# Running the first half of a GEGLU FFN beside a block convolution, with streamed weights, batched complex products and a second PSUM buffer for FFN2

## Chip, cores, metric

One core of one Trainium2 chip. The metric is the device time of one execution in microseconds (us); where several runs of a kernel are quoted, it is their median. Runs are marked fast or slow by their own spread; only fast ones are compared, except one single run (e3_serial_b) whose state is unknown and which is named as such.

## The reference, cut to what matters

The inputs are bf16: u of 2048 tokens by D = 640 channels, SSM parameters of 640 by 128, FFN weights with F = 1728. The FFN reads u too; its own x is not used.

```python
g = sigmoid((u * gate_w).sum(-1, keepdims=True))
# a: state-space layer as a long convolution
K = real(einsum("dn,dnl,dn->dl", C, exp(dt * A * l), dt * B))    # 640 x 2048
a = irfft(rfft(pad(u)) * rfft(pad(K)))[:2048] + u * Dskip
# b: GEGLU feed-forward
b = (gelu(u @ w_gate) * (u @ w_up)) @ w_down                     # tanh form of gelu
return g * a + (1 - g) * b
```

## The kernel before

It has five stages, one after another: the SSM kernel K (80 pieces); DFT tables and the forward DFT of K in four blocks of 512; the convolution, block by block in the frequency domain; FFN1 (56 tiles of up to 128 features by 512 tokens); FFN2 with the final mix (16 tiles of 128 tokens). A complex spectrum has nine planes of 640 columns: real and imaginary planes alternate, and plane 8 is the Nyquist plane. The parts that the change and the argument touch:

```python
K_sb = kpool.tile([128, TC, D], BF16, name="K_sb")            # K stays in SBUF
Kf = big.tile([128, NB, NT, D], BF16, name="Kf")              # and so do all its spectra
...
for c in range(NB):                                           # convolution, output block c of 4
    ub = upool.tile([128, 4, D], BF16, name="ub")
    nc.sync.dma_start(out=ub[:], in_=u2[c * S:(c + 1) * S, :].rearrange("(t p) d -> p t d", p=128))
    ...
    fwd_block(ub, lambda k: k, Uf, c)                         # DFT: TensorE, copied out by ScalarE
    for i in range(c + 1):
        j = c - i
        for t in range(4):                                    # one complex plane at a time
            Ur = Uf[:, i, 2 * t, :]; Ui = Uf[:, i, 2 * t + 1, :]
            Kr = Kf[:, j, 2 * t, :]; Ki = Kf[:, j, 2 * t + 1, :]
            ...                                               # 8 products and sums of 128x640
    ...                                                       # Mc = Sprev * sgn + Sc, VectorE
    for mo in range(4):
        pY = psY.tile([128, D], FP32, name="pY")              # inverse DFT of Mc on TensorE
        ...
        nc.vector.tensor_tensor(out=a_sb[:, tcx, :], in0=a_sb[:, tcx, :], in1=pY[:], op=ALU.add)

# FFN: everything is loaded only here, in tiles that reuse the convolution's memory
xT = fp.tile([128, nkt, L], BF16, name="xT")
for kt in range(nkt):
    nc.sync.dma_start_transpose(out=xT[:, kt, :], in_=u2[:, kt * 128:(kt + 1) * 128])
nc.sync.dma_start(out=Wg[:], in_=B_w_gate.rearrange("(k p) f -> p k f", p=128))
nc.sync.dma_start(out=Wu[:], in_=B_w_up.rearrange("(k p) f -> p k f", p=128))
...
for ft in range(nft):                                         # FFN1
    for tq in range(L // 512):
        ...                                                   # 5 + 5 matmuls, then
        nc.scalar.copy(out=Gs[:fsz], in_=pGt[:fsz])
        nc.scalar.copy(out=Us[:fsz], in_=pUt[:fsz])
        nc.vector.tensor_tensor(out=q[:fsz], in0=Gs[:fsz], in1=Gs[:fsz], op=ALU.mult)
        nc.vector.tensor_scalar(out=q[:fsz], in0=q[:fsz], scalar1=0.044715, scalar2=1.0, op0=ALU.mult, op1=ALU.add)
        nc.vector.tensor_tensor(out=q[:fsz], in0=q[:fsz], in1=Gs[:fsz], op=ALU.mult)
        nc.scalar.activation(out=sg[:fsz], in_=q[:fsz], func=ACT.Sigmoid, scale=GELU_C)
        nc.vector.tensor_tensor(out=sg[:fsz], in0=sg[:fsz], in1=Gs[:fsz], op=ALU.mult)
        nc.vector.tensor_tensor(out=HT[:fsz, ft, toks], in0=sg[:fsz], in1=Us[:fsz], op=ALU.mult)
for tt in range(TC):                                          # FFN2
    pD = psF.tile([128, D], FP32, name="pD", bufs=1)
    ...                                                       # 28 matmuls, b_sb on ScalarE, mix on VectorE
```

Of the kernel before, what the change touches and what calls it, by code (L numbers as in the profile page):

```python
# [9 lines left out]
ALU = mybir.AluOpType  # L10
ACT = mybir.ActivationFunctionType
FP32 = mybir.dt.float32
# [10 lines left out]
def kernel(  # L23
# [73 lines left out]

    kctx = ExitStack()
    kctx.__enter__()
    kpool = kctx.enter_context(tc.tile_pool(name="kpool", bufs=1))  # L100
    K_sb = kpool.tile([128, TC, D], BF16, name="K_sb")

    with ExitStack() as k1:
# [171 lines left out]
        def kgen_contract_C(hb, tabs):  # L275
# [11 lines left out]
            for r in range(4):  # L287
                nc.sync.dma_start(out=K_sb[32 * r:32 * (r + 1), :, cslc],
                                  in_=K0[:, r:X2:4, :])
# [28 lines left out]
    if "K" in dbg:  # L318
        nc.sync.dma_start(out=dbg["K"].rearrange("(j p) d -> p j d", p=128), in_=K_sb[:])
    persist = kctx.enter_context(tc.tile_pool(name="persist", bufs=1))  # L320
    a_sb = persist.tile([128, TC, D], BF16, name="a_sb")
    g_sb = persist.tile([128, TC], BF16, name="g_sb")
    with ExitStack() as k2:
# [7 lines left out]

        dctx = ExitStack()
# [60 lines left out]
        dctx.__exit__(None, None, None)  # L393
        Uf = big.tile([128, NB, NT, D], BF16, name="Uf")
        Kf = big.tile([128, NB, NT, D], BF16, name="Kf")
        dchs = [(0, 512), (512, D - 512)] if D > 512 else [(0, D)]

        def fwd_block(src, kidx, spec, b):
            for mt in range(NT):
                pU = psT.tile([128, D], FP32, name="pU")  # L400
                for (d0, dn) in dchs:
                    for k in range(4):
                        nc.tensor.matmul(pU[:, d0:d0 + dn], lhsT=FW[:, k, mt, :], rhs=src[:, kidx(k), d0:d0 + dn],  # L403
                                         start=(k == 0), stop=(k == 3))
                nc.scalar.copy(out=spec[:, b, mt, :], in_=pU[:])  # L405

        for b in range(NB):
            fwd_block(K_sb, lambda k, b=b: 4 * b + k, Kf, b)

        upool = k2.enter_context(tc.tile_pool(name="ublk", bufs=2))  # L410
        spool = k2.enter_context(tc.tile_pool(name="sacc", bufs=2))
        psY = k2.enter_context(tc.tile_pool(name="psinv", bufs=2, space=bass.MemoryType.PSUM))
        Sprev = None
        for c in range(NB):
            ub = upool.tile([128, 4, D], BF16, name="ub")
            nc.sync.dma_start(out=ub[:], in_=u2[c * S:(c + 1) * S, :].rearrange("(t p) d -> p t d", p=128))
            for k in range(4):
                nc.vector.tensor_tensor(out=a_sb[:, 4 * c + k, :], in0=ub[:, k, :], in1=dsk[:], op=ALU.mult)
            fwd_block(ub, lambda k: k, Uf, c)
            Sc = spool.tile([128, NT, D], BF16, name="Sc")  # L420
            first = True
            for i in range(c + 1):
                j = c - i
                for t in range(4):
                    Ur = Uf[:, i, 2 * t, :]
                    Ui = Uf[:, i, 2 * t + 1, :]
                    Kr = Kf[:, j, 2 * t, :]
                    Ki = Kf[:, j, 2 * t + 1, :]
                    Sr = Sc[:, 2 * t, :]
                    Si = Sc[:, 2 * t + 1, :]  # L430
                    tmp = wk.tile([128, D], BF16, name="ptmp")
# [16 lines left out]
                U8 = Uf[:, i, 8, :]  # L448
                K8 = Kf[:, j, 8, :]
                S8 = Sc[:, 8, :]  # L450
                tmp8 = wk.tile([128, D], BF16, name="ptmp8")
                if first:
                    nc.vector.tensor_tensor(out=S8, in0=U8, in1=K8, op=ALU.mult)
                else:
                    nc.vector.tensor_tensor(out=tmp8[:], in0=U8, in1=K8, op=ALU.mult)
                    nc.vector.tensor_tensor(out=S8, in0=S8, in1=tmp8[:], op=ALU.add)
                first = False
            if c > 0:
                Mc = spool.tile([128, NT, D], BF16, name="Mc", bufs=1)
                for mt in range(NT):  # L460
                    nc.vector.scalar_tensor_tensor(out=Mc[:, mt, :], in0=Sprev[:, mt, :],  # L461
                                                   scalar=sgn[:], in1=Sc[:, mt, :],
                                                   op0=ALU.mult, op1=ALU.add)
            else:
                Mc = Sc
            for mo in range(4):
                pY = psY.tile([128, D], FP32, name="pY")
                for (d0, dn) in dchs:
                    for kt in range(NT):
                        nc.tensor.matmul(pY[:, d0:d0 + dn], lhsT=FI[:, kt, mo, :], rhs=Mc[:, kt, d0:d0 + dn],  # L470
                                         start=(kt == 0), stop=(kt == NT - 1))
                tcx = 4 * c + mo
                nc.vector.tensor_tensor(out=a_sb[:, tcx, :], in0=a_sb[:, tcx, :], in1=pY[:], op=ALU.add)
            Sprev = Sc

    if "a" in dbg:
        nc.sync.dma_start(out=dbg["a"].rearrange("(t p) d -> p t d", p=128), in_=a_sb[:])
    with ExitStack() as k3:
        fp = k3.enter_context(tc.tile_pool(name="ffn", bufs=1))
        fwk = k3.enter_context(tc.tile_pool(name="fwork", bufs=2))  # L480
        psF = k3.enter_context(tc.tile_pool(name="psffn", bufs=2, space=bass.MemoryType.PSUM))
        psC = k3.enter_context(tc.tile_pool(name="psconst", bufs=1, space=bass.MemoryType.PSUM))

        nkt = D // 128
        nft_full = F // 128
        f_last = F - nft_full * 128
        nft = nft_full + (1 if f_last else 0)
        xT = fp.tile([128, nkt, L], BF16, name="xT")
        for kt in range(nkt):
            nc.sync.dma_start_transpose(out=xT[:, kt, :], in_=u2[:, kt * 128:(kt + 1) * 128])  # L490
        Wg = fp.tile([128, nkt, F], BF16, name="Wg")
        nc.sync.dma_start(out=Wg[:], in_=B_w_gate.rearrange("(k p) f -> p k f", p=128))
        Wu = fp.tile([128, nkt, F], BF16, name="Wu")
        nc.sync.dma_start(out=Wu[:], in_=B_w_up.rearrange("(k p) f -> p k f", p=128))
# [4 lines left out]
        gwc = fp.tile([128, nkt], BF16, name="gwc")  # L499
        nc.sync.dma_start(out=gwc[:], in_=gate_w.rearrange("(k p) -> p k", p=128))  # L500

        pG = psC.tile([128, TC], FP32, name="pgate")
        for tt in range(TC):
            for kt in range(nkt):
                nc.tensor.matmul(pG[:, tt:tt + 1], lhsT=xT[:, kt, tt * 128:(tt + 1) * 128], rhs=gwc[:, kt:kt + 1],
                                 start=(kt == 0), stop=(kt == nkt - 1))
        glog = fwk.tile([128, TC], BF16, name="glog")
        nc.scalar.copy(out=glog[:], in_=pG[:])
        nc.scalar.activation(out=g_sb[:], in_=glog[:], func=ACT.Sigmoid)
        if "g" in dbg:  # L510
            nc.sync.dma_start(out=dbg["g"].rearrange("(t p) -> p t", p=128), in_=g_sb[:])
        if "Uf" in dbg:
            pass

        HT = fp.tile([128, nft, L], BF16, name="HT")
        GELU_C = 2.0 * math.sqrt(2.0 / math.pi)
        for ft in range(nft):
            fsz = 128 if ft < nft_full else f_last
            f0 = ft * 128
            for tq in range(L // 512):  # L520
                toks = slice(tq * 512, (tq + 1) * 512)
                pGt = psF.tile([128, 512], FP32, name="pGt")
                pUt = psF.tile([128, 512], FP32, name="pUt")
                for kt in range(nkt):
                    nc.tensor.matmul(pGt[:fsz, :], lhsT=Wg[:, kt, f0:f0 + fsz], rhs=xT[:, kt, toks],  # L525
                                     start=(kt == 0), stop=(kt == nkt - 1))
                for kt in range(nkt):
                    nc.tensor.matmul(pUt[:fsz, :], lhsT=Wu[:, kt, f0:f0 + fsz], rhs=xT[:, kt, toks],  # L528
                                     start=(kt == 0), stop=(kt == nkt - 1))
                Gs = fwk.tile([128, 512], BF16, name="Gs")  # L530
                nc.scalar.copy(out=Gs[:fsz], in_=pGt[:fsz])  # L531
                Us = fwk.tile([128, 512], BF16, name="Us")
                nc.scalar.copy(out=Us[:fsz], in_=pUt[:fsz])  # L533
                q = fwk.tile([128, 512], BF16, name="q")
                nc.vector.tensor_tensor(out=q[:fsz], in0=Gs[:fsz], in1=Gs[:fsz], op=ALU.mult)
# [56 lines left out]
```

## Time and profile before

Four runs before the prediction: 834.88 us (833.73 to 836.83). The table by stage, the chain and their reading stand in the prediction. In short: the convolution is full of VectorE work, FFN1 of TensorE work, and between them lies a hole of 26.6 us in which x and the FFN weights are loaded.

A row of the table by stage reads: stretch, its length, the busy time of TensorE, its weight loads, VectorE, ScalarE and GpSimd (instructions in brackets), the granted TensorE clock, the DMA share, GB/s. In the traces PE is TensorE, DVE is VectorE, ACT is ScalarE, and SPq is the queue of DMA issues on SyncE.

### The profile page before, as it was taken

The page shows a single profiled execution, that of the slowest core. Times are in us where ns is not written, and L with a number is a line of the kernel's source. Part 1 is how long each engine was busy: PE and PEld are TensorE (multiplying, and loading weights), DVE is VectorE, ACT ScalarE, POOL GpSimd, SP SyncE. Part 2 cuts the span into 40 slices and gives each one's busy share as a digit, 9 for nine tenths or more (in the row PEclk, how much of TensorE's full clock was granted, in tenths as well). Part 3 has the DMA queues.
Part 4 walks back from the last instruction along what each step waited for, and adds up shares of the span by engine and source line. Part 5 has one row for each costly group of instructions (what it writes and reads, how often), then busy time and mean ns, then how long its engine had stood idle before and what let it go on. Part 6 is the DMA issues. An engine that isn't in the chain of part 4 may idle for free.

```text
span 833.4 us, 9851 instructions
## 1 busy us (share of the span) xinstructions
PE 509.7 (61%) x3597; PEld 252.2 (30%) x3652; DVE 670.7 (80%) x1580; ACT 456.6 (55%) x560; POOL 5.8 (1%) x25
## 2 busy tenths in 40 slices
PE   0056545755675565316979960500539999998886
PEld 0021313322332323303545530200214444444443
DVE  6979899899999898699979999999417788884333
ACT  1139999999999999525753420000016766661111
POOL 2000000000000000000000000000000000000000
PEclk9998779786976796667999995755859999999999
DMA  2000000000000000100011100000391000000000
GB/s 63 0 0 0 1 1 14 13 4 10 14 13 1 13 13 0 27 13 1 2 64 32 33 1 0 0 0 0 73 322 52 1 1 1 0 1 32 33 32 31
DMA packets 44656, 19.06 MB, mean 23 GB/s; under 512 B 37248, under 2 KB 43328, under 8 KB 44608
## 3 DMA queue, kind: packets, MB, share of 16 engines
q1 hardware_dynamic: 44608, 18.44, 8.6%
q8 instruction: 28, 0.46, 0.2%
q14 instruction: 20, 0.16, 0.1%
HBM read 9.91 MB, written 2.62 MB: 15 GB/s over the span
## 4 chain that ended last, share of the span: by engine, by line
DVE 40%; ACT 35%; PE 17%; issue 3%; DMA 2%; SPq 2%; ACTq 0%; DVEq 0%
PE pD L549 8%; ACT c L267 4%; ACT e L254 4%; ACT c L265 4%; ACT p L269 4%; ACT sg L539 4%; DVE sg L540 3%; DVE Mc L461 3%; DVE q L537 2%; ACT p L268 2%; ACT c L266 2%; PE pY L470 2%; DVE HT L541 2%; DMA Wu<-in_B_w_up_dram 2%; ACT L249 2%
## 5 line engine op out<-in xcount | busy, mean ns | idle before, releaser
L531 ACT CAST Gs<-pGt 128x512 bf16<-128x512 f32 (+1 forms) x56 | 32.2, 577 | 128.3 <-PE pGt L525 127.9
L257 DVE TENSOR_SCALAR kM<-pph 128x512 f32<-128x512 f32 x120 | 79.5, 682 | 22.3 <-PE pph L253 14.5
L525 PE MATMUL pGt<-xT,Wg 128*128 128x512 bf16 (+1 forms) x269 | 70.2, 386 | 24.9 <-DMA Wg<-in_B_w_gate_dram 22.1
L470 PE MATMUL pY<-Mc,FI 128*128 128x128 bf16 (+1 forms) x211 | 36.7, 324 | 78.8 <-DVE Mc L461 78.3
L258 DVE SCALAR_TENSOR_TENSOR p<-kM,pph 128x512 bf16<-128x512 f32 x120 | 77.8, 675 | 0.2
L549 PE MATMUL pD<-Wd,HT 128*128 128x128 bf16 (+3 forms) x440 | 68.0, 298 | 13.1 <-ACT b_sb L552 12.6
L253 PE MATMUL pph<-RX,b_bf 128*128 128x512 bf16 x80 | 36.3, 461 | 60.4 <-DVE p L258 60.2
L528 PE MATMUL pUt<-xT,Wu 128*128 128x512 bf16 (+1 forms) x280 | 69.2, 379 | 0.4 <-ACT Us L533 0.4
L403 PEld LDWEIGHTS <-FW 128*128 128x128 bf16 x576 | 46.5, 101 | 70.4 <-ACT FW L385 26.9
L283 PEld LDWEIGHTS <-c 128*32 128x32 bf16 x640 | 44.7, 104 | 62.5 <-DVE K L285 37.7
L283 PE MATMUL psK<-c,c 128*32 128x64 bf16 x640 | 52.2, 204 | 17.6 <-DVE c L272 12.1
L403 PE MATMUL pU<-K_sb,FW 128*128 128x128 bf16 (+1 forms) x282 | 43.7, 311 | 28.1 <-ACT FW L385 25.3
L539 ACT ACTIVATE sg<-q 128x512 bf16<-128x512 bf16 (+1 forms) x56 | 35.2, 629 | 35.5 <-DVE q L537 35.1
L470 PEld LDWEIGHTS <-FI 128*128 128x128 bf16 x288 | 23.6, 101 | 102.0 <-DVE Mc L461 49.2
L285 DVE CAST K<-psK 32x512 bf16<-32x512 f32 x80 | 51.2, 670 | 3.3 <-PE psK L284 2.9
L556 DVE TENSOR_TENSOR diff<-a_sb,b_sb 128x640 f32<-128x640 bf16 x16 | 13.2, 824 | 50.4 <-ACT b_sb L552 50.4
L284 PE MATMUL psK<-p,p 128*32 128x64 bf16 x640 | 51.5, 203 | 3.1 <-DVE p L273 3.1
L549 PEld LDWEIGHTS <-HT 128*128 128x128 bf16 x448 | 34.7, 97 | 46.6 <-issue 22.3
L405 ACT CAST Uf<-pU 128x640 bf16<-128x640 f32 x36 | 24.9, 692 | 42.9 <-PE pU L403 42.9
L254 ACT ACTIVATE e<-pa 128x512 bf16<-128x512 f32 x80 | 44.5, 595 | 6.6 <-PE pa L252 6.3
L552 ACT CAST b_sb<-pD 128x640 bf16<-128x640 f32 x16 | 11.0, 690 | 66.4 <-PE pD L549 66.4
L284 PEld LDWEIGHTS <-p 128*32 128x32 bf16 x640 | 45.1, 104 | 6.3 <-issue 6.3
(167 smaller groups left out, 1150.0 us busy)
## 6 DMA issues: line engine op xcount, KB each, us to landing
K_sb<-K SPq DMA_DIRECT2D x40, 64.0 KB, 2.3
ub<-in_A_u_dram SPq DMA_DIRECT2D x4, 640.0 KB, 4.2
out_dram<-o_sb SPq DMA_DIRECT2D x16, 160.0 KB, 1.8
Wg<-in_B_w_gate_dram SPq DMA_DIRECT2D x1, 2160.0 KB, 8.6
Wu<-in_B_w_up_dram SPq DMA_DIRECT2D x1, 2160.0 KB, 13.5
Wd<-in_B_w_down_dram SPq DMA_DIRECT2D x1, 2080.0 KB, 19.0
dsk<-in_A_Dskip_dram SPq DMA_DIRECT2D x1, 160.0 KB, 3.6
Are<-in_A_A_re_dram SPq DMA_DIRECT2D x1, 160.0 KB, 3.7
```

The source lines that it names most:

```text
L254: nc.scalar.activation(out=et[:, :, xs], in_=pa[:], func=ACT.Exp)
L257: nc.vector.tensor_scalar(out=kM[:], in0=tau_src, scalar1=MAGIC, scalar2=None, op0=ALU.add)
L258: nc.vector.scalar_tensor_tensor(out=pt[:, :, xs], in0=kM[:], scalar=-MAGIC, in1=tau_src, op0=ALU.add, op1=ALU.subtract)
L283: nc.tensor.matmul(psK[:, ci, :], lhsT=c1[:, dl, :], rhs=c2[:, dl, :], start=True, stop=False)
L284: nc.tensor.matmul(psK[:, ci, :], lhsT=p1[:, dl, :], rhs=p2[:, dl, :], start=False, stop=True)
L285: nc.vector.tensor_copy(out=K0[:, :, ch8 * 8:(ch8 + 1) * 8], in_=psK[:].rearrange("p c x -> p x c"))
L403: nc.tensor.matmul(pU[:, d0:d0 + dn], lhsT=FW[:, k, mt, :], rhs=src[:, kidx(k), d0:d0 + dn], start=(k == 0), stop=(k == 3))
L470: nc.tensor.matmul(pY[:, d0:d0 + dn], lhsT=FI[:, kt, mo, :], rhs=Mc[:, kt, d0:d0 + dn], start=(kt == 0), stop=(kt == NT - 1))
L525: nc.tensor.matmul(pGt[:fsz, :], lhsT=Wg[:, kt, f0:f0 + fsz], rhs=xT[:, kt, toks], start=(kt == 0), stop=(kt == nkt - 1))
L528: nc.tensor.matmul(pUt[:fsz, :], lhsT=Wu[:, kt, f0:f0 + fsz], rhs=xT[:, kt, toks], start=(kt == 0), stop=(kt == nkt - 1))
L539: nc.scalar.activation(out=sg[:fsz], in_=q[:fsz], func=ACT.Sigmoid, scale=GELU_C)
L549: nc.tensor.matmul(pD[:, d0:d0 + dn], lhsT=HT[:fsz, ft, toks], rhs=Wd[:fsz, ft, d0:d0 + dn], start=(ft == 0), stop=(ft == nft - 1))
```

## The change

The intent is to place the TensorE-bound FFN1 beside the VectorE-bound convolution, and so to hide its matmuls and its load. What is needed for that is memory: K and its spectra go to DRAM and come back block by block; the FFN weights are loaded in tiles, once for each quarter of the tokens; H, the result of FFN1, goes to DRAM as well. Besides, the four planes of a complex product are done in one instruction, and FFN2 gets two PSUM buffers. The core of the diff (cuts marked with ...):

```diff
+    K_dram = dram.tile([TC, 128, D], BF16, name="K_dram")
+    Kf_dram = dram.tile([NB, 128, NT, D], BF16, name="Kf_dram")
+    HT_dram = dram.tile([F, L], BF16, name="HT_dram")
-    K_sb = kpool.tile([128, TC, D], BF16, name="K_sb")
...
-                for t in range(4):
-                    Ur = Uf[:, i, 2 * t, :]
...
+        def conv_gen():
...
+                RE = slice(0, 8, 2)
+                IM = slice(1, 8, 2)
+                for i in range(c + 1):
+                    Kfj = kfs.tile([128, NT, D], BF16, name="Kfj", tag="kf")
+                    nc.sync.dma_start(out=Kfj[:], in_=Kf_dram[j])
+                    Ur = Uf[:, i, RE, :]
+                    ...                    # the same products, on 128 x 4 x 640
+                    yield
...
+        def ffn1_gen():
+            for tq in range(L // 512):
+                ...                        # xq: transposed tokens of this quarter; gate
+                yield
+                for ft in range(nft):
+                    if ft % 2 == 0:
+                        ...                # wg2, wu2: 640 x 256 of each weight, two buffers
+                    ...                    # 5 + 5 matmuls into one pGU, one copy of 1024 to GU
+                    ...                    # the same five VectorE instructions and the sigmoid
+                    nc.sync.dma_start(out=HT_dram[f0:f0 + fsz, toks], in_=ht[:fsz])
+                    yield
+        run_interleaved([conv_gen(), two_at_a_time(ffn1_gen())])
...
         for tt in range(TC):
-            pD = psF.tile([128, D], FP32, name="pD", bufs=1)
+            HTs = hp.tile([128, nft, 128], BF16, name="HTs")
+            ...                            # HTs from HT_dram, 256 B runs
+            pD = psD.tile([128, D], FP32, name="pD")      # psD has bufs=2
```

`run_interleaved` takes one step of each generator in turn, so two FFN1 tiles stand beside each step of the convolution. The compiler's scheduler orders each engine's instructions from there.

## The prediction

> **What bounds the kernel now.** I read the page's busy row and slices first, then the busy time of every engine by stage, then the chain, then the groups of the stages that the change touches, and last the DMA issues.
>
> ```profile
> PE 509.7 (61%) x3597; PEld 252.2 (30%) x3652; DVE 670.7 (80%) x1580; ACT 456.6 (55%) x560; POOL 5.8 (1%) x25
> DVE 40%; ACT 35%; PE 17%; issue 3%; DMA 2%; SPq 2%; ACTq 0%; DVEq 0%
> ```
>
> The first line is the share of busy time, the second the chain that ended last. No engine bounds the whole span. The stages run one after another, each with its own limit, which the table by stage shows (stretch, its length, busy us per engine, TensorE clock, DMA share, GB/s):
>
> ```profile
> 0.00:354.60 354.60, 185.59 (x1681) 90.24 (x1700) 307.05 (x429) 288.45 (x229) 5.76 (x25) 0.82 0.07 11
> 354.60:425.30 70.70, 43.69 (x282) 23.53 (x288) 70.25 (x477) 40.01 (x107) 0.00 (x0) 0.81 0.03 5
> 425.30:595.80 170.50, 86.33 (x566) 46.23 (x576) 161.89 (x364) 25.60 (x37) 0.00 (x0) 0.76 0.05 16
> 595.80:622.40 26.60, 4.60 (x14) 1.78 (x15) 1.91 (x4) 1.16 (x2) 0.00 (x0) 0.62 0.97 272
> 622.40:752.20 129.80, 125.70 (x644) 57.85 (x654) 101.99 (x277) 90.99 (x171) 0.00 (x0) 1.00 0.05 16
> 752.20:833.40 81.20, 63.77 (x413) 32.52 (x419) 27.61 (x33) 10.41 (x16) 0.00 (x0) 1.00 0.09 33
> ```
>
> Row 1 makes the SSM kernel K (ScalarE and VectorE bound). Row 2 makes the DFT tables (VectorE 70.25 of 70.70) with the forward DFT of K beside them on TensorE. Row 3 is the block convolution: VectorE is busy 161.89 of 170.50 and TensorE only half. Row 4 is a hole: every engine waits for x and the FFN weights, DMA share 0.97. Row 5 is FFN1, bound by TensorE (125.70 of 129.80) with VectorE at 101.99. Row 6 is FFN2, where TensorE waits. So a VectorE-bound stage stands before a TensorE-bound one, with a load between.
>
> The groups of the convolution and of FFN1 that I count with:
>
> ```profile
> L272 DVE TENSOR_TENSOR c<-c,e 128x4096 bf16<-128x4096 bf16 x10 | 22.9, 2289 | 4.0 <-ACT c L267 3.9
> L270 DVE TENSOR_TENSOR c<-c,e 128x2048 bf16<-128x2048 bf16 x10 | 12.2, 1221 | 2.3 <-ACT c L266 1.8 <-ACT e L249 0.5
> L446 DVE TENSOR_TENSOR ptmp<-Uf,Kf 128x640 bf16<-128x640 bf16 x24 | 11.1, 481 | 0.0
> L461 DVE SCALAR_TENSOR_TENSOR Mc<-Sc,sgn 128x640 bf16<-128x640 bf16 x27 | 21.8, 876 | 0.0
> L525 PE MATMUL pGt<-xT,Wg 128*128 128x512 bf16 (+1 forms) x269 | 70.2, 386 | 24.9 <-DMA Wg<-in_B_w_gate_dram 22.1 <-ACT Gs L531 2.0
> L552 ACT CAST b_sb<-pD 128x640 bf16<-128x640 f32 x16 | 11.0, 690 | 66.4 <-PE pD L549 66.4
> ```
>
> And three pieces of the timeline: two products that start 0.80 us apart per pair, and one FFN2 tile, where TensorE idles 0.82 us for its only pD buffer.
>
> ```profile
> 491.50 0.80 DVE ptmp L440 x2
> 788.22 4.28 PE L549 MATMUL pD<-Wd,HT 128*128 128x512 bf16 x27 [0.82 <-ACT b_sb L552]
> 829.86 0.88 DVE L558 SCALAR_TENSOR_TENSOR o_sb<-diff,g_sb,b_sb 128x640 bf16<-128x640 f32 x1
> ```
>
> **What the Trainium skill says.** (1) "VectorE: DVE Perf Modes", The perf-mode tier table: a bf16 tensor_tensor reaches two elements per cycle and no more. The trace agrees: from 128x2048 to 128x4096 the time grows by 1068 ns for 2048 elements, 0.521 ns each. (2) Same page, What auto-detection actually checks: this mode asks for 16-bit tensors with step 1. The new products read four planes of 640 with a stride between; the inner step stays 1, so I keep the mode, though no instruction of this trace has that shape. (3) "TensorE: Matmul & The Clock Gate", Part 1: idle stretches throttle the array, sustained work releases it. The trace agrees: 0.76 granted in the convolution, 1.00 in FFN1. (4) "DMA: Bandwidth & Descriptors", Specifications: transfers want runs of at least 512 B. The new weight tiles have 512 B runs, the new HTs loads 256 B. No transfer of these shapes is in the trace; the nearest is K_sb, 64 KB in 128 B runs, 2.3 us to landing.
>
> **The change part by part.**
>
> *Stages 1 and 2* keep their VectorE and ScalarE work and order. K goes to DRAM in place of SBUF and is read back in blocks; the read (two DMAs of a few us after the last K piece) lies under the 20 us in which the tables are not ready anyway. The first four FFN1 tiles can use TensorE's idle time there, and the first u block no longer has a late load (4.0 us of VectorE idle today). I leave 425.3 us as the start of the merged stage.
>
> *VectorE work of the convolution.* Today in starts-apart: 288 products at 0.402 us are 115.8; 16 skip products 6.5; 16 Nyquist products 6.4; 27 Mc at 0.796 (nine took 7.16) are 21.5; 16 additions of pY at about 0.73 are 11.8; sum 162.0, and the row says 161.89. So starts-apart, not durations, is the right unit. An instruction of 640 costs 0.333 us of elements and 0.069 us fixed. Batched by four: 2560 x 0.521 + 0.069 = 1.40 us against 4 x 0.402 = 1.61. So 72 products cost 101, plus about 0.1 us for the forty or so that now follow the one they depend on (the unbatched code alternated two chains): 105. Four skip products 5.6, six Mc of 2560 at 2.80 and three of 640 at 0.80 are 19.2, the rest 18.2. Sum 148: batching gains 14 us.
>
> *FFN1 elementwise.* The same five VectorE instructions for 56 tiles: 102 + 1 us for those outside the row = 103, slightly less when interleaving removes small gaps, 101. ScalarE has one copy of 1024 in place of two of 512 and stays far from a bound (about 56 x 1.0 + 56 x 0.63 + 36 x 0.69 = 116 us).
>
> *Merged stage.* VectorE: 148 + 101 = 249 us. TensorE at full clock: FFN1 and gate 126, forward and inverse DFT of u about 20 per block at the measured 0.21 us per 512-column matmul and 0.07 per 128-column one, so 80; sum 206, under VectorE's 249. Today these rows take 170.5 + 26.6 + 129.8 = 326.9 us, so full overlap would save 78 us: 27 from the hole, 14 from batching, the rest by hiding FFN1's TensorE time.
>
> Overlap is not full. The compiled order shows engines in fixed sequence; where the inverse DFT waits for Mc, FFN matmuls behind it wait too; the sync queue is one sequence of HT writes, weight loads and Kf loads. Today's convolution has 5% VectorE idle and FFN1 waits 20 us in all for its sigmoid. In the changed order some 14 FFN tiles remain after the last convolution work; there the chain of square, sigmoid, product paces at about 2.5 us a tile against 1.8 of work: 10 us. For waits before that I take 20 us (8%). Merged stage: 249 + 10 + 20 = 279 us, ending at 704.
>
> *DMA.* New traffic: weights four times 4.4 MB, ten Kf blocks of 1.47 MB, 5.9 MB of Kf out, H 7 MB out and in, near 45 MB. Row 4 moved 272 GB/s; over 279 us the need is some 150. Weight tiles are prefetched one pair ahead. Not a bound, unless order makes it one.
>
> *FFN2.* Now 5.10 us a tile (4.28 and the 0.82 wait). With two pD buffers TensorE runs on: 14 x 0.216 + 14 x 0.073 = 4.05 us. But H comes back from DRAM in 256 B runs, 432 KB a tile, with two buffers; I estimate from the 2.3 us of K_sb and the 3 us that 416 KB would take at half of row 4's rate that a load takes some 4.5 to 5 us, a little over a tile's matmuls, so 4.4 us a tile: 70 us. The tail after the last matmul stays 5 us. TensorE finishes FFN1 about 3 us before VectorE, which the first tile uses.
>
> Sum: 704 - 3 + 70 + 5 = 776; I say **775 us**, 7% faster.
>
> **The rivals.** *A: the strided batched products lose the two-per-cycle mode.* Then 72 of them cost about 1.33 us more each (1.04 ns per element as in Mc), +96: 870 us, slower. Against it: inner step 1 and 16-bit. Under 4%. *B: one in-order sync queue and in-order engines turn overlap into waits*: Kf loads that wait for a freed slot hold back HT writes and weights, and ht has only two buffers. Two to three us at each of ten Kf loads and four inverse DFTs adds 25 to 40: 800 to 815 us. For it: 190 queue entries instead of 29. Against: VectorE work paces the stage and each stream has slack of several tiles. *C: H loads bind FFN2* at 5.5 us or more a tile: +18, 793 us. For: 256 B runs, 1728 per tile. Against: the 128 B runs of K_sb were quick. *D: overlap is near perfect*: 425 + 249 + 70 = 745 to 750 us.
>
> **Range and chances.** Half of B or all of C lands near 795, D near 748. Range 750 to 804. Faster by over 2% needs under 818, which B and C together barely break; slower needs A. Chances 0.95, 0.03, 0.02.
>
> **What would show it right or wrong.** The hole with DMA share near 1 must be gone. From 425 to about 704 VectorE should be busy about 90% with 245 to 252 us of work, TensorE about 75% at a clock nearer 1. Batched products should show about 1.49 us mean duration (2.8 means rival A). VectorE waits for ScalarE or for DMA on ht over 30 us mean rival B. FFN2 tiles should come 4.1 to 4.6 us apart with TensorE waiting for HTs by DMA at most a little; over 5 is rival C. Stages 1 and 2 should end within 3 us of today; if the tables start late because K's round trip or a buffer holds them up, the prediction is wrong there.

## The result, and the profile after

| | us, median | range | runs | after or variant / before |
|---|---|---|---|---|
| before | 835.08 | 833.73 to 836.83 | 13 | |
| after | 751.99 | 750.66 to 753.93 | 8 | 0.9007, 95% interval 0.8997 to 0.9018 |

A ratio is the mean time of one kernel's fast runs over the mean of the other's fast runs of the same rounds, so not quite the ratio of the medians quoted. The kernel after is 10% faster; 775 was predicted, with 750 to 804 as the range.

The page of the kernel after, busy time of each engine and the chain that ended last:

```profile
PE 510.6 (68%) x3597; PEld 250.4 (33%) x3652; DVE 641.8 (86%) x1334; ACT 454.2 (61%) x507; POOL 5.8 (1%) x25
ACT 35%; DVE 33%; PE 22%; DMA 4%; issue 3%; SPq 1%; ACTq 0%; DVEq 0%
```

TensorE, with the same matmuls, has the same busy time as before; VectorE's fell by 29 us in 246 fewer instructions. The 83 us did not come from less work alone, and the table by stage says where they came from. Kernel after, columns as before:

```profile
0.00:354.00 354.00, 182.84 (x1681) 89.39 (x1700) 307.15 (x432) 288.47 (x229) 5.76 (x25) 0.83 0.08 15
354.00:424.00 70.00, 52.18 (x327) 27.18 (x335) 69.93 (x475) 42.48 (x109) 0.00 (x0) 0.93 0.53 166
424.00:680.00 256.00, 212.47 (x1180) 102.28 (x1199) 236.73 (x397) 112.20 (x154) 0.00 (x0) 0.93 0.59 171
680.00:749.40 69.40, 63.10 (x413) 31.57 (x421) 27.99 (x34) 11.07 (x16) 0.00 (x0) 0.98 0.52 131
```

The first two rows are as long as before. The third takes the place of convolution, hole and FFN1: 256 us for 326.9 (VectorE's last FFN1 instruction ends at 680.7, so it is 257 when read to there). In it VectorE is busy 92% of the time and TensorE 83%, with DMA at 0.59 all along in place of one burst at 0.97. FFN2 went from 81.2 to 69.4 us.

VectorE's waits in these stages (line and tile waited with, what it waited for: us in total, times, longest), kernel before, from 425.3 to 752.2 us:

```profile
DVE q L535 <- ACT Gs L531: 26.8, 5, 24.2
DVE sg L540 <- ACT sg L539: 20.4, 37, 0.7
```

and kernel after, from 424 to 680 us:

```profile
DVE q L535 <- ACT GU L531: 6.6, 11, 1.4
DVE sg L540 <- ACT sg L539: 6.5, 10, 1.1
DVE ht L542 <- DMA HT_dram<-ht: 0.9, 3, 0.4
```

The hole was the 24.2 us wait of the first list: VectorE waits for ScalarE's first copy, which waits for matmuls, which wait for weights. It is gone. The waits for the sigmoid fell from 37 to 10, where a product of the convolution often stands in the place of the wait; with FFN1 alone again (e3_serial_b, below) there are 26.

A batched product as a group, and four successive VectorE instructions of the kernel after (start, duration, engine, line), two of FFN1 and two of the convolution:

```profile
L453 DVE TENSOR_TENSOR ptmp<-Uf,Kfj 128x2560 bf16<-128x2560 bf16 x6 | 8.9, 1481 | 1.7 <-ACT Uf L413 1.7
```

```profile
604.24 0.42 DVE L540 TENSOR_TENSOR sg<-sg,GU 128x512 bf16<-128x512 bf16 x1
604.58 1.48 DVE L456 TENSOR_TENSOR Sc<-Sc,ptmp 128x2560 bf16<-128x2560 bf16 x1
605.99 0.42 DVE L542 TENSOR_TENSOR ht<-sg,GU 128x512 bf16<-128x512 bf16 x1
606.32 1.48 DVE L457 TENSOR_TENSOR ptmp<-Uf,Kfj 128x2560 bf16<-128x2560 bf16 x1
```

A product takes 1.48 us by its duration, and the next instruction starts 1.40 or 1.41 us after it. The small ones take 0.42 and are followed after 0.34. Line 542 needs the result of line 540 and line 457 overwrites what line 456 read, but each pair has another instruction in between, and no start is late.

FFN2 in the kernel after: ScalarE's copies out of PSUM mark the tiles, and the last line, from the list of DMA issues, gives the loads of H (count, size, median us from issue to landing):

```profile
701.70 0.69 ACT L579 CAST b_sb<-pD 128x640 bf16<-128x640 f32 x1 [3.53 <-PE pD L576]
705.92 0.69 ACT L579 CAST b_sb<-pD 128x640 bf16<-128x640 f32 x1 [3.53 <-PE pD L576]
```

```profile
HTs<-HT_dram SPq DMA_DIRECT2D x16, 416.0 KB, 3.8
```

A tile every 4.22 us where it was 5.10, and a load lands in less time than a tile takes.

### The profile page after: what moved, and what is told of

Read it like the earlier page. It is cut to its first block, busy times and chain, and to the rows that moved or that the text cites.

```text
span 749.4 us, 9833 instructions
## 1 busy us (share of the span) xinstructions
PE 510.6 (68%) x3597; PEld 250.4 (33%) x3652; DVE 641.8 (86%) x1334; ACT 454.2 (61%) x507; POOL 5.8 (1%) x25
## 4 chain that ended last, share of the span: by engine, by line
ACT 35%; DVE 33%; PE 22%; DMA 4%; issue 3%; SPq 1%; ACTq 0%; DVEq 0%
PE pD L576 7%; ACT c L269 5%; ACT e L256 5%; ACT c L267 5%; ACT p L271 5%; PE pU L484 4%; ACT p L270 2%; ACT c L268 2%; PE pGU L525 2%; PE pGU L528 2%; ACT L251 2%; DVE q L535 2%; ACT L268 2%; DVE nfq L351 1%; DVE q L537 1%
## 5 line engine op out<-in xcount | busy, mean ns | idle before, releaser
L531 ACT CAST GU<-pGU 128x1024 bf16<-128x1024 f32 (+1 forms) x56 | 56.5, 1008 | 74.6 <-DVE ht L542 38.3
L525 PE MATMUL pGU<-xq,wg 128*128 128x512 bf16 (+1 forms) x269 | 77.4, 410 | 26.5 <-ACT GU L531 21.3
L528 PE MATMUL pGU<-xq,wu 128*128 128x512 bf16 (+1 forms) x278 | 72.5, 391 | 0.1
L576 PE MATMUL pD<-Wd,HTs 128*128 128x128 bf16 (+3 forms) x440 | 67.6, 299 | 1.0 <-DMA HTs<-HT_dram 0.5
L411 PE MATMUL pU<-kb,FW 128*128 128x128 bf16 (+1 forms) x281 | 41.6, 299 | 19.2 <-DMA kb<-K_dram 9.1
L525 PEld LDWEIGHTS <-wg 128*128 128x128 bf16 (+1 forms) x280 | 28.2, 104 | 61.5 <-issue 33.1
L576 PEld LDWEIGHTS <-HTs 128*128 128x128 bf16 x448 | 33.7, 97 | 34.9 <-issue 10.8
L484 PE MATMUL pU<-Mc,FI 128*128 128x128 bf16 (+1 forms) x213 | 35.8, 321 | 13.1 <-DVE Mc L475 12.5
L254 PE MATMUL pa<-RX,a_bf 128*128 128x512 bf16 x80 | 33.1, 423 | 15.0 <-ACT e L256 12.8
```

Source lines behind the costliest of these rows:

```text
L411: nc.tensor.matmul(pU[:, d0:d0 + dn], lhsT=FW[:, k, mt, :], rhs=src[:, k, d0:d0 + dn], start=(k == 0), stop=(k == 3))
L484: nc.tensor.matmul(pY[:, d0:d0 + dn], lhsT=FI[:, kt, mo, :], rhs=Mc[:, kt, d0:d0 + dn], start=(kt == 0), stop=(kt == NT - 1))
L525: nc.tensor.matmul(pGU[:fsz, 0, :], lhsT=wg[:, kt, :fsz], rhs=xq[:, kt, :], start=(kt == 0), stop=(kt == nkt - 1))
L528: nc.tensor.matmul(pGU[:fsz, 1, :], lhsT=wu[:, kt, :fsz], rhs=xq[:, kt, :], start=(kt == 0), stop=(kt == nkt - 1))
L531: nc.scalar.copy(out=GU[:fsz], in_=pGU[:fsz])
L576: nc.tensor.matmul(pD[:, d0:d0 + dn], lhsT=HTs[:fsz, ft, :], rhs=Wd[:fsz, ft, d0:d0 + dn], start=(ft == 0), stop=(ft == nft - 1))
```

## The experiments

Eleven kernels gave a correct result on the chip; one more run repeats a variant for its profile. The ratio is always to the kernel before, run in the same rounds. Differences of under 2% (e2, e3, e5) are read here because the 95% intervals of their ratios, given in brackets, leave out 1. First the three parts of the change, each undone alone in the kernel after or done alone in the kernel before.

### Products not batched (e1_unbatched)

```diff
-                    Ur = Uf[:, i, RE, :]          # ... products on 128 x 4 x 640
+                    for t in range(4):
+                        Ur = Uf[:, i, 2 * t, :]   # ... products on 128 x 640, as before the change
```

> The changed kernel with the 72 spectral products of 4x640 split again into 288 of 640; all else as changed. Theory (overlap and batching add up; VectorE paces the merged stage, and its fixed 0.069 us per instruction is what batching saves): 288 x 0.402 - 72 x 1.40 = 15 us more VectorE work, nearly all of it on the path: 762 to 770 us. Rival (the batching matters little, since the merged stage waits for other things): under 757 us.

Measured: 763.1 us (761.91 to 763.39), ratio 0.914 [0.912, 0.916]: 11 us slower than the kernel after. Its stretch of convolution and FFN1:

```profile
424.00:693.10 269.10, 216.50 (x1225) 104.15 (x1224) 253.91 (x629) 116.02 (x159) 0.00 (x0) 0.92 0.58 168
```

The time lies where the theory put it. VectorE's work is 254 us in place of 237, and the stretch, to VectorE's last FFN1 instruction, 269 in place of 257. So batching saves 17 us of work here, of which 11 to 12 show in the time.

### Batching alone (e2_before_batched)

The reverse edit, in the kernel before.

> The kernel before with only the products batched by four. Theory: the convolution stage is VectorE bound, so 10 to 15 us of its 170 go: 820 to 825 us; the merged stage showed starts 1.40 us apart even for an instruction that needs the one just before it, but always with another between, and here there are none between, so up to 0.1 us each on some 40 to 60 of them may stay. Rival (batching is only worth something when independent FFN work fills the gaps between dependent products): 828 to 835 us.

Measured: 829.51 us (827.42 to 830.26), ratio 0.994 [0.992, 0.996], in the rival's range. The convolution of this kernel, and two of VectorE's waits in it:

```profile
425.00:587.70 162.70, 86.52 (x565) 46.05 (x566) 146.81 (x146) 24.91 (x36) 0.00 (x0) 0.76 0.05 16
DVE Sc L434 <- ACT Uf L405: 6.9, 1, 6.9
DVE a_sb L474 <- PE pY L471: 7.3, 5, 1.7
```

VectorE's work falls by 15 us, from 161.9 to 146.8, but only some 5 us come out. The first batched product needs four real planes of Uf, the last of which is the seventh to come from ScalarE, where the unbatched one needed only the first; VectorE now waits 6.9 us there, where it did not wait before. For the inverse DFT's results it waits 7.3 us, where it was 4.6. The saving is real; alone it is half given back, because this large instruction waits for the last of its inputs and there is no other work to put in front of it. In the kernel after, VectorE waits for planes of Uf only once, 1.7 us.

### FFN1 after the convolution instead of beside it (e3_serial, e3_serial_b, e10_serial_deep)

All the rest of the change stays: streaming, batching, two pD buffers.

```diff
-        run_interleaved([conv_gen(), two_at_a_time(ffn1_gen())])
+        run_interleaved([conv_gen()])
+    with ExitStack() as k2b:              # FFN1's pools open once the convolution's are closed
+        ...
+        run_interleaved([ffn1_gen()])
```

> The changed kernel with the same batched products, the same streaming FFN1 and the same FFN2, but FFN1's pools opened after the convolution's are closed, so that FFN1 runs after the convolution, not beside it. Theory (overlap is the largest part): convolution 148 to 155 us, a short wait of some 6 us for the first x and weight tile, FFN1 bound by TensorE at about 126 to 130 us: the stage goes from 257 to 280 to 290 us: 775 to 787 us. Rival (what paid was the streaming of weights that took the 26.6 us hole away, and VectorE is the bound either way): 752 to 762 us.

Measured: the three fast runs are 830.19, 830.62 and 827.93 us, ratio 0.994 [0.991, 0.996]. The expectation of 775 to 787 missed by some 45 us: this variant is 78 us slower than the kernel after, and not the 30 or so that were expected. The first profile fell in an execution of 1755 us (last section) and explains nothing, so the same kernel was sent again for its profile, and beside it one with deeper buffers:

```diff
-        wtp = k2.enter_context(tc.tile_pool(name="wts", bufs=2))
-        fwk = k2.enter_context(tc.tile_pool(name="felt", bufs=2))
+        wtp = k2b.enter_context(tc.tile_pool(name="wts", bufs=4))
+        fwk = k2b.enter_context(tc.tile_pool(name="felt", bufs=4))
```

> The serial variant again, for a profile of an undisturbed execution: its first profile fell in an execution of 1755 us in which every matmul took four times as long. Time about 830 us as before. Theory: the streamed FFN1, alone, is bound by the chain of one tile (weight matmuls, copy, three VectorE instructions, sigmoid, two VectorE instructions) through two buffers of each temporary: tiles 2.9 us or more apart where VectorE has 1.66 us of work per tile, with VectorE's waits put down to the sigmoid (ScalarE) in most of 56 tiles; FFN1 alone then takes 160 us or more, and the convolution stage alone about 160 us. Rival: the convolution stage is what is long (190 us or more; batched products that wait for the planes and for the inverse transform's results), and FFN1's tiles come about 2.2 us apart. Second rival: FFN1 waits for its weight tiles; then PE's waits name wg2 or wu2.

> The serial variant with four buffers instead of two for the FFN1 temporaries and for the weight tiles. Theory (the two-deep chain makes the serial FFN1 slow): tiles come close to VectorE's or ScalarE's work per tile, about 2.0 us, and the time falls from 830 to 780-795 us. Rival (a wait that has nothing to do with these buffers: the in-order instruction streams, in which VectorE's product after the sigmoid holds the next tile's squares back, or the convolution stage itself): at most 8 us are won, 822-830 us; then the overlap with the convolution is what hides the chain, whatever the buffers.

Measured: e3_serial_b 826.76 us (one run, state unknown, like the fast ones of e3_serial); e10_serial_deep 816.89 us (815.96 to 818.42), ratio 0.979 [0.977, 0.982], which neither its theory (780 to 795) nor its rival (822 to 830) had. The convolution and FFN1 of e3_serial_b, one row each:

```profile
424.00:600.80 176.80, 88.63 (x601) 47.05 (x599) 145.79 (x122) 26.01 (x40) 0.00 (x0) 0.77 0.31 108
600.80:746.00 145.20, 126.96 (x620) 56.46 (x620) 104.77 (x280) 89.61 (x117) 0.00 (x0) 0.95 0.75 197
```

FFN1 alone is bound by TensorE, as it was before the change: busy 127 of 145 us. The expectation of e3_serial had that right; none of the three theories written for the rerun names it. FFN1's tiles start every 2.37 us (55 intervals from 601.2 to the last tile's 731.6), not every 2.9. TensorE waits for weight tiles 5.5 us in this row, the second rival's wait, but no more. With four buffers they come every 2.25 us, close to the ten matmuls' own 2.16, and ScalarE waits for TensorE at nearly every tile. ScalarE's wait in e10_serial_deep, 600.8 to 735 us:

```profile
ACT GU L535 <- PE pGU L532: 39.1, 52, 5.9
```

So the buffers are worth 10 us there against e3_serial_b, 13 against the fast runs of e3_serial, and no more: below them is TensorE.

Two moments of the kernel before, and one of e3_serial_b, show where TensorE changes from stage to stage:

```profile
617.80 6.15 PE L525 MATMUL pGt<-xT,Wg 128*128 128x512 bf16 x19 [22.09 <-DMA Wg<-in_B_w_gate_dram]
747.11 4.29 PE L549 MATMUL pD<-Wd,HT 128*128 128x512 bf16 x27
749.82 2.72 PE L575 MATMUL pD<-Wd,HTs 128*128 128x512 bf16 x6 [15.89 <-DMA HTs<-HT_dram]
```

Read by TensorE, both kernels up to FFN2's first matmul:

| | before, us | e3_serial_b, us |
|---|---|---|
| convolution, to its last matmul | 170.4 | 166.5 |
| gap until FFN1's first matmul | 22.1 | 10.7 |
| FFN1's matmuls | 129.4 | 132.7 |
| gap until FFN2's first matmul | 0 | 15.9 |
| sum | 321.8 | 325.8 |

In the last gap the last tiles pass through VectorE, H is written and its first block comes back. That is, streaming and batching without overlap lose 4 us in this stretch: they shorten the hole and lose more at the end. That e3_serial is still a little faster than the kernel before fits its second pD buffer, worth 12 to 13 us (below). VectorE has 145 us of work in the 166.5 us of this convolution and waits 8.1 us for the inverse DFT, 6.8 for the first block of u and 5.7 for planes of Uf; in the merged stretch these waits are 2.1, none and 1.7. The overlapped kernel takes 253 us from 424 to FFN1's last matmuls, in which the start and nearly all the end lie beside other work as well.

The serial kernel also shows what happens to VectorE when it has one stream only. Three successive products of e3_serial_b, each dependent on the one in front:

```profile
474.57 1.49 DVE L458 TENSOR_TENSOR Sc<-Sc,ptmp 128x2560 bf16<-128x2560 bf16 x1
476.09 1.49 DVE L459 TENSOR_TENSOR ptmp<-Uf,Kfj 128x2560 bf16<-128x2560 bf16 x1
477.62 1.49 DVE L460 TENSOR_TENSOR Sc<-Sc,ptmp 128x2560 bf16<-128x2560 bf16 x1
```

They start 1.52 and 1.53 us apart, not 1.40. Most products escape this even here, as another product or addition stands between: of the 74 instructions of 2560 columns that are followed without a wait, 14 are followed only after 1.49 us or more (counted in the trace; in the kernel after, one of 75). In FFN1 it is the rule: 125 of 177 instructions of 512 columns with two inputs are followed after 0.42 us or more in place of 0.33 to 0.40; in the kernel after, 31 of 172. VectorE's work of the two stages is 145.8 + 104.8 = 250.6 us, against 237 with both streams interleaved.

### One and two pD buffers (e4_one_pD, e5_before_two_pD)

```diff
-        psD = k3.enter_context(tc.tile_pool(name="psffn2", bufs=2, space=bass.MemoryType.PSUM))
+        psD = k3.enter_context(tc.tile_pool(name="psffn2", bufs=1, space=bass.MemoryType.PSUM))
```

> The changed kernel with one pD buffer in place of two. Theory (the second buffer removed the 0.8 us wait at each of 16 tiles, and loads of H from DRAM of 3.8 us keep up with 4.1 us of matmuls): 13 us slower, 763 to 767 us. Rival (H loads would bind FFN2 anyway, with two buffers or one): under 757 us.

Measured: 765.01 us (764.29 to 769.07), ratio 0.918 [0.915, 0.920]: 13 us slower than the kernel after. TensorE's wait in FFN2 is back, once for each tile but one:

```profile
PE pD L576 <- ACT b_sb L579: 12.3, 15, 0.8
```

The time lies in the theory's range. The other way round, two buffers of FFN2's own in the kernel before, in a pool opened after FFN1's is closed:

```diff
+        psD = k3.enter_context(tc.tile_pool(name="psffn2", bufs=2, space=bass.MemoryType.PSUM))
-            pD = psF.tile([128, D], FP32, name="pD", bufs=1)
+            pD = psD.tile([128, D], FP32, name="pD")
```

> The kernel before with only FFN2 changed: its PSUM pool opened after FFN1's is closed, with two pD buffers. Theory: 15 waits of 0.82 us go, 12 to 16 us: 819 to 824 us. Rival (something else paces the tiles, for instance the weight loads of TensorE): 830 us or more.

Measured: 822.46 us (822.28 to 825.96), ratio 0.987 [0.984, 0.989], 12 us faster than the kernel before. This part of the change is independent of the rest and is worth the same in both kernels, and its tiles, with H in SBUF, come 4.22 us apart, as they do in the kernel after with H from DRAM. So bringing H back costs FFN2 nothing once it runs.

### More FFN1 tiles beside each step (e6_ratio)

```diff
         def two_at_a_time(g):
+            n = 0
             for _ in g:
                 next(g, None)
+                n += 1
+                if n % 3 == 0:
+                    next(g, None)
                 yield
```

> The changed kernel with 7 FFN tiles to 3 convolution steps in place of 6, so that FFN1 ends with the convolution. Theory (the last 27 us, FFN tiles alone, leave VectorE idle for 7.6 us in the chain of square, sigmoid, product, and interleaving hides that): 4 to 8 us faster, 744 to 748 us. Rival (the idle time only moves to another place, to where TensorE waits for the convolution): 750 to 754 us.

Measured: 755.83 us (753.7 to 756.21), ratio 0.905 [0.903, 0.907]: 4 us slower, where 4 to 8 us faster was expected and the rival had 750 to 754. The stretch did end some 5 us earlier, at 676, since fewer tiles were left for the end. Yet TensorE then waited for H. TensorE's last FFN1 matmuls and its first of FFN2, and the issue of that tile's load:

```profile
669.52 1.24 PE L528 MATMUL pGU<-xq,wu 128*64 128x512 bf16 x5
677.85 0.58 PE L580 MATMUL pD<-Wd,HTs 128*128 128x512 bf16 x1 [7.08 <-DMA HTs<-HT_dram]
```

```profile
673.40 0.58 SPq L572 DMA_DIRECT2D HTs<-HT_dram  x1
```

The load is issued at 673.40, behind two writes of H which stand in front of it in the same queue, before a load of w_down, and need VectorE's results. In the kernel after it was issued at 663.5. So the tail of FFN1 tiles alone, which the prediction put at 10 us, is partly a cost and partly cover for the change to FFN2: shortening it at one end uncovers the other.

### Less VectorE work, deeper buffers (e7_square_act, e8_felt3, e9_square_felt4, e11_poly_act)

If VectorE bounds the merged stretch, work taken off it must show. The square goes to ScalarE:

```diff
-                    nc.vector.tensor_tensor(out=q[:fsz], in0=Gs, in1=Gs, op=ALU.mult)
+                    nc.scalar.activation(out=q[:fsz], in_=Gs, func=ACT.Square)
```

> The changed kernel with the square G*G moved from VectorE to ScalarE (56 instructions of about 0.34 us between starts, 19 us; ScalarE is busy 112 of 256 us). Theory (VectorE paces the merged stage): 10 to 18 us faster, 734 to 742 us. Rival (the stage is paced by latency through ScalarE, PSUM and buffers): the square on ScalarE makes that chain longer by 0.4 to 0.6 us a tile, 750 to 770 us.

Measured: 742.8 us (742.04 to 743.2), ratio 0.890 [0.888, 0.891]: 9 us faster than the kernel after, just short of the 10 that the theory had as its least, and far from the rival's 750 to 770. Its stretch, and VectorE's two main waits in it:

```profile
424.00:673.50 249.50, 211.77 (x1197) 102.65 (x1219) 218.67 (x353) 144.84 (x212) 0.00 (x0) 0.95 0.60 179
```

```profile
DVE sg L540 <- ACT sg L539: 13.9, 14, 1.8
DVE q L536 <- ACT q L535: 7.1, 6, 2.2
```

VectorE has 18 us less to do; about half of it turns into waits, most of them for ScalarE. Three buffers in place of two for the FFN1 temporaries, with the square left on VectorE:

```diff
-        fwk = k2.enter_context(tc.tile_pool(name="felt", bufs=2))
+        fwk = k2.enter_context(tc.tile_pool(name="felt", bufs=3))
```

> The changed kernel with three buffers in place of two for GU, q, sg and ht. Theory (VectorE is 92 percent busy in the merged stage, and what it waits for is mostly the sigmoid and the PSUM copy in the tail, which deeper buffers help a little): 2 to 6 us faster, 746 to 750 us. Rival (ScalarE waits 38 us for ht to free a GU buffer and TensorE 21 us for ScalarE; these waits set the pace): 8 us or more faster.

Measured: 750.32 us (747.72 to 752.42), ratio 0.899 [0.896, 0.903]: 1 to 2 us, at the limit of what these runs tell; the rival, 8 us or more, is out. With both, and four buffers:

> The kernel after with the square on ScalarE and four buffers for the FFN1 temporaries. Theory: the square on ScalarE freed 18 us of VectorE and got 9 of them, the rest lost in waits of VectorE for ScalarE (about 21 us); deeper buffers take a part of these waits back, as they took 1 to 2 us with the square on VectorE: 735-741 us. Rival: the waits are of the order in which the tiles' instructions stand on each engine (five VectorE instructions behind a sigmoid that has only just been started), which buffers don't change: 742 us within 1.5.

Measured: 730.37 us (727.32 to 732.2), ratio 0.875 [0.872, 0.878], below the range that the theory gave, and the rival is out. Deeper buffers that were worth nearly nothing with the square on VectorE are worth 12 us with the square on ScalarE. But three were tried there and four here, and no run has four with the square on VectorE; that VectorE's gaps make the difference is likely, not shown. The stretch:

```profile
424.00:661.00 237.00, 209.17 (x1201) 99.79 (x1199) 216.35 (x346) 140.31 (x206) 0.00 (x0) 0.95 0.63 188
```

Last, the multiply-and-add behind the square goes to ScalarE too:

```diff
-                    nc.vector.tensor_scalar(out=q[:fsz], in0=q[:fsz], scalar1=0.044715, scalar2=1.0, op0=ALU.mult, op1=ALU.add)
+                    nc.scalar.activation(out=q[:fsz], in_=q[:fsz], func=ACT.Copy, bias=1.0, scale=0.044715)
```

> The square and the following multiply-and-add both on ScalarE, four buffers for the FFN1 temporaries. Theory (the merged stage is still bound by VectorE's work, and ScalarE, busy 140 of 237 us, has room): VectorE gives up 56 instructions of about 0.22 us, 12 us, ScalarE takes 56 of 0.63 us, 35 us, and is then busy 175 us; two thirds of the 12 us show: 720-726 us against 730. Rival (both engines are now near balance, and each tile's chain through ScalarE, with copy, square, multiply-and-add and sigmoid at 0.6 to 1.0 us each, about 2.9 us a tile beside the convolution's plane copies, paces the tiles and also the stretch of FFN1 tiles at the end): no gain, 729-736 us.

Measured: 721.47 us (720.22 to 722.93), ratio 0.864 [0.863, 0.866]. This is the fastest version tried, 30 us below the kernel after. Its stretch:

```profile
424.00:650.00 226.00, 202.92 (x1178) 98.92 (x1199) 202.88 (x285) 167.53 (x256) 0.00 (x0) 0.97 0.66 195
```

VectorE and TensorE are both busy 203 of 226 us. Each step agrees with VectorE as what mainly bounds the kernel after in this stretch: 18 us and then 13 to 14 us less work gave 9 us at two buffers, 22 with deeper ones, and 9 more. The last step uses the two engines evenly, so another move off VectorE would meet TensorE; no run here tried one.

## Why the prediction was right

The direction and the mechanism held, the size roughly (7% against 10%), and the range narrowly: 752 lies 2 us above its lower end. By its own steps:

- **The start of the merged stage** was left at 425.3 us; it is 423.9. K's way through DRAM cost nothing there: TensorE waited 9.1 us for its first block, under VectorE's tables.
- **The two-per-cycle mode of strided products** held: 1.48 us by duration, as the prediction gave it. Rival A is out.
- **VectorE's work** was put at 249 us, with 245 to 252 as a sign of being right; it is 237. The term that was too high is dependence. The prediction charged the batched products 0.1 us for forty dependent followers, 4 us, and took FFN1's tiles near what they cost alone, 101 us. In the merged kernel the other stream stands between dependent instructions: products start 1.40 us apart, and what is left for FFN1 is 93 us (an estimate: 237 less 101 for products and 43 for the rest), or 1.66 us a tile. So 4 us of the 12 are the charge on the products and 8 are FFN1's. The serial variant is the check: with one stream the late starts are there, above all in FFN1, and its 250.6 us are the predicted sum to within 2. In that closeness is some luck: its convolution is 2 us below the predicted 148 and its FFN1 4 us above 101.
- **Waits**: 30 us were allowed, 10 of them at the end; VectorE stood idle 20 us, some 8 of them in the last 27 us, where FFN1 tiles were alone. Rival B (25 to 40 us more in an in-order queue) did not come in this form; e6_ratio shows the same queue doing it, 7 us at one place, when the order of issue is less lucky.
- **The merged stage** then took 257 us and not 279: 12 us of work and 10 of waits. This is the step that missed, in size: it makes 22 of the 27 us between the prediction's sum, 776, and the profiled span, 749.4. FFN2 makes 3 and the earlier start 1.
- **FFN2**: 4.4 us a tile predicted, 4.2 measured; the load of H took 3.8 us and not 4.5 to 5. Rival C is out.
- **The DMA traffic** was summed wrongly: the terms given make 52 MB with H counted out and in, not 45. The page of the kernel after has 69.1 MB in its queue against 18.4, 50.7 more. Nothing rested on it; the DMA share of the merged stretch is 0.59.
- **Rival D**, near-perfect overlap at 745 to 750 us, is close to the result by its number. It had the prediction's VectorE work, 249 us, and no waits; the true sum is less work and some waits.
- **The split of the gain**: the prediction gave 27 us of the 78 to the hole, 14 to batching and the rest to hiding. The runs, each undoing one part, give 11 to batching, 13 to the second pD buffer and 75 to 78 to the overlap (65 if the serial variant has four buffers). They add to more than the 83 gained, since parts depend on each other: batching alone is worth 5 and not 11, and the shorter hole of the serial variant is lost again at its end.

The serial experiment is where the expectations fell short. FFN1 was not the miss: it was expected at 126 to 130 us, bound by TensorE, and its matmuls took 132.7. The convolution alone took 166.5 us and not 148 to 155, since VectorE's waits were left out; the load in front of FFN1 took 10.7 us and not 6; and the 15.9 us between FFN1 and FFN2 were not in the sum at all. The rerun then looked for the time in a slow chain of FFN1's tiles, which was not there.

## What to carry to other kernels

When the busy table shows a VectorE-bound stage next to a TensorE-bound one with a load between, the sum of the fuller engine's work over both is the floor, and interleaving them can come within a tenth of it; what it costs is memory, and the DMA traffic that pays for the memory cost little here while it was spread out: in the merged stretch TensorE waits for it 4.6 us and VectorE 0.9. Batching or prefetching that gains little by itself may pay in full once another stream fills the waits, so test such parts inside the merged form too. After the merge, rank the engines again: moving two small operations from the full engine to a free one, with deeper buffers, gave another 30 us.

## What the Trainium skill lacked or had wrong

- "VectorE: DVE Perf Modes", The DRAIN you can't avoid, reports eight copies that took as long with a semaphore after each as with one after the last, and so that the semaphore costs nothing extra there. It gives no cost for an instruction that really waits for its predecessor, and that cost is not zero: in these runs an instruction that depends on the one directly in front starts 0.12 to 0.13 us later than one that does not (1.52 to 1.53 us against 1.40 for 128x2560; 0.46 against 0.34 for 128x512), and one independent instruction in between removes this.
- "TensorE: Matmul & The Clock Gate", Seeing it yourself, warns of a clock gate stuck at a quarter rate for 50 us and more and of unreliable records. One execution of e3_serial was wholly like that: 1755 us where the same kernel took 828 to 831, a 512-column matmul of FFN1 1102 to 1106 ns by its mean duration where e3_serial_b has 384 to 386, about 0.88 us of TensorE's busy time for each (245.3 us for 280) where 0.216 is usual, and a granted clock recorded as 1.00 throughout. Whether the gate was its cause is open; the time and the durations show it, the clock column does not.
- No page that I read has the duration of a bf16 tensor_tensor over four separate planes: 1.48 us for 4 x 640 columns, with 1.40 from start to start, so the stride between planes costs nothing that these runs show.
